# A late store sent in parts of 93, 32 and 3 partitions, and final waits in the order of issue

## The chip, the cores and the metric

The kernel runs on one NeuronCore of one Trainium2 chip. The time is the device time of one execution in microseconds (us); the lower it is, the better. The core has five engines with their own instruction streams: TensorE (PE in the profile, with PEld for its weight loads), VectorE (DVE), ScalarE (ACT), GpSimd (POOL) and SyncE (SP). SP does no arithmetic: here it issues transfers between HBM and the core's own memory, and waits for them. The transfers themselves are carried by 16 DMA engines.

## What is computed

A recurrence along a sequence, and on its result a mixture of eight low-rank adapters of which each row uses two:

```python
# a, b: (8, 6400, 128) float32
for t in range(S):
    h = a[:, t] * h + b[:, t]
    out[:, t] = h
x = out.reshape(51200, 128)

logits = x @ w_gate                                  # 8 experts
topk = np.argpartition(-logits, 2, axis=1)[:, :2]
...                                                  # softmax over the two: w
for e in range(8):
    for k in range(2):
        mask = topk[:, k] == e
        delta[mask] += w[mask, k, None] * ((x[mask] @ A[e]) @ B[e])   # A[e]: 128x16, B[e]: 16x128
return x + delta
```

Inputs `a` and `b` are 26.2 MB each, and the output is 26.2 MB.

## The kernel before

The 51,200 rows are cut into 100 chunks of 512 (`NCH = 100`, `C = 512`). For each chunk PE turns the rows of `a` and `b` so that time runs along the free dimension (line 567), DVE runs the recurrence over it (line 618), PE multiplies the result with gate and `A` (line 638), ACT copies these out of PSUM (line 644), a group of units gets its gate values (lines 671 to 694), DVE or POOL scale the products with them (lines 712 to 716), PE turns them (line 725), ACT or DVE copy them out (lines 731, 734), PE adds up the result (lines 739, 740), and ACT copies it into the buffer `outt` (line 749). From there SP stores it to HBM (line 784).

`outt` holds 72 blocks of 128 rows, which is 18 chunks: chunk c + 18 is copied to where chunk c was, so that copy waits until the store of chunk c has landed. All stores but the last four take two chunks at a time, 512 KB, and are called by the first: `st0`, `st2`, up to `st94`. The last four chunks, 96 to 99, are stored singly, 256 KB each. In `outt` and in HBM a store has 128 partitions; each has two pieces of 2 KB in a store of two chunks and one piece in a single one. `st68` stores chunks 68 and 69.

Each transfer adds 16 to a semaphore when it has landed. Stores of two chunks use nine semaphores in turn, `st0` to `st8` by their place in `outt`; the single ones use `stx0` to `stx3`. `st68` uses the semaphore `st7`, which `st86` uses again 18 chunks later.

The order of the instructions on each engine is worked out before the program is built: `Program.schedule` takes the operations in the order of a rank (a base, a template and a nudge by hand), with a duration for each. SP's own order is part of it: loads and stores stand in one stream, 48 loads of 512 KB of each input behind some smaller ones at the head. The last load is issued at 164.2 us; behind it stand twenty stores, `st64` to `st94` and then chunks 97, 98, 99 and 96. `st68` is the third of them.

When a store goes out in several parts, `SPLIT` gives the numbers of partitions for it by its first chunk; `send` (line 783) then issues one transfer for each part, all to the same semaphore, and `parts` makes the waits count 16 for each. In the kernel before `SPLIT` is empty. At the end of SP's stream (lines 838 to 840) it waits for each store semaphore to reach its full count, in the order in which the semaphores were made: `st0` to `st8`, then `stx0` to `stx3`.

Of the kernel before, what the change touches and what calls it, by code (L numbers as in the profile page):

```python
# [121 lines left out]
HEAD = 4  # L122
TAIL = 0
STORE_TAIL = [1, 1, 1, 1]
SPLIT = {}
TEMPLATE = {
    "la": [-7.837, -6.512, -2.793],
    "lb": [-6.969, -4.142, -2.441],
# [195 lines left out]
def bass_associative_scan_2x2__then__mixture_of_adapters_kernel(  # L324
# [65 lines left out]
    for u0, n in groups:  # L390
        nb = sum(m for _, m in units[u0 : u0 + n])
        if pos + nb > NZ:
            pos = 0
        for u in range(u0, u0 + n):
            zpos[u] = pos
            pos += units[u][1]

    with ExitStack() as stack:
# [41 lines left out]
        P = Program()  # L440
# [6 lines left out]
        s_dma = {}  # L447
# [46 lines left out]
        o_Z, o_ze, o_mu, o_T, o_te, o_D, o_oe, o_st = {}, {}, {}, {}, {}, {}, {}, {}  # L494
# [279 lines left out]
        def store(c, m):  # L774
# [4 lines left out]
            view = outt[:, q : q + m * J, :].rearrange("p (h j) d -> p h j d", j=J)  # L779
            cuts = SPLIT.get(c, [128])  # L780
            lows = [sum(cuts[:i]) for i in range(len(cuts))]
# [39 lines left out]
        def run(name, handle):  # L821
            eng[name] = handle
            for op in P.order[name]:
                for key, v in waits[op.i]:
                    handle.wait_ge(s_eng[key] if key in s_eng else s_dma[key], v)
                inst = op.emit()
                if op.sem is None:
                    inst.then_inc(s_eng[name], 1)
                else:
                    for part in inst if op.parts > 1 else [inst]:  # L830
                        part.then_inc(s_dma[op.sem], 16)
# [3 lines left out]
        @block.sync  # L835
        def _(sp):
            run("sp", sp)
            for key in s_dma:
                if key.startswith("st"):
                    sp.wait_ge(s_dma[key], 16 * sum(o.parts for o in o_st.values() if o.sem == key))  # L840

        @block.gpsimd
        def _(pool):
# [41 lines left out]
```

## Time and profile before

| what | us |
| --- | --- |
| median of three runs | 204.07 |
| lowest and highest of them | 203.96, 204.29 |
| the profiled execution, its own time | 204.2 |
| its span, from the first instruction to the last | 202.4 |
| PE, DVE, ACT, POOL busy in it | 182.1, 176.2, 172.6, 139.0 |

The span is what the trace covers; the rest of the profiled execution's time lies before the first and after the last instruction. A line with a line number, an engine and tiles (`L784 SPq DMA_DIRECT2D out_dram<-outt`) is a group of like instructions; SPq marks work of SP's queue, that is, issuing. "DMA to landing" is the time from the start of an issue until the transfer's semaphore has its full count. In the windows the columns after the times are the busy times of the engines with counts, then the granted clock of TensorE, the mean busy share of the 16 DMA engines (it can pass 1.00, since a packet's time can overlap the next one's) and the GB/s that they moved.

### The profile page before, as it was taken

The page shows a single profiled execution, that of the slowest core. Times are in us where ns is not written, and L with a number is a line of the kernel's source. Part 1 is how long each engine was busy: PE and PEld are TensorE (multiplying, and loading weights), DVE is VectorE, ACT ScalarE, POOL GpSimd, SP SyncE. Part 2 cuts the span into 40 slices and gives each one's busy share as a digit, 9 for nine tenths or more (in the row PEclk, how much of TensorE's full clock was granted, in tenths as well). Part 3 has the DMA queues.
Part 4 walks back from the last instruction along what each step waited for, and adds up shares of the span by engine and source line. Part 5 has one row for each costly group of instructions (what it writes and reads, how often), then busy time and mean ns, then how long its engine had stood idle before and what let it go on. Part 6 is the DMA issues. An engine that isn't in the chain of part 4 may idle for free.

```text
span 202.4 us, 7462 instructions
## 1 busy us (share of the span) xinstructions
PE 182.1 (90%) x3120; PEld 157.8 (78%) x3120; DVE 176.2 (87%) x291; ACT 172.6 (85%) x314; POOL 139.0 (69%) x176
## 2 busy tenths in 40 slices
PE   6878999999999999999999998987898998989870
PEld 6768787888888888888888887876887887877750
DVE  0579899999999999999999999887888998999960
ACT  2448899999999999999999997987797988978882
POOL 1015559998788898888888889796878897471000
PEclk9999999999999999999999999999999999999998
DMA  7999999999999999999999999999999999999994
GB/s 186 365 387 390 407 410 406 402 412 406 406 415 410 410 410 411 417 409 407 411 414 405 411 408 417 408 411 416 406 413 412 411 414 410 404 401 373 347 359 149
DMA packets 30993, 79.26 MB, mean 392 GB/s; under 512 B 3696, under 2 KB 3824, under 8 KB 30960
## 3 DMA queue, kind: packets, MB, share of 16 engines
q1 hardware_dynamic: 29488, 78.39, 98.7%
q10 hardware_dynamic: 1472, 0.40, 0.9%
q8 instruction: 25, 0.41, 0.8%
q14 instruction: 8, 0.07, 0.1%
HBM read 52.56 MB, written 26.21 MB: 389 GB/s over the span
## 4 chain that ended last, share of the span: by engine, by line
PE 23%; DMA 20%; DVE 19%; issue 1%; ACT 1%; SPq 0%; DVEq 0%
DMA b_tm<-in_b_dram 13%; DVE xT L618 9%; DMA a_tm<-in_a_dram 7%; PE pA L567 5%; PE pZ L638 4%; PE pB L567 4%; PE pO L725 3%; PE pO L739 3%; DVE zwT L734 3%; PE pO L740 3%; DVE zw L716 3%; DVE g L693 1%; ACT zwT L731 1%; ACT outt L749 1%; DVE m L672 1%
## 5 line engine op out<-in xcount | busy, mean ns | idle before, releaser
L618 DVE TENSOR_TENSOR_SCAN xT<-a_st,xT,pB 128x512 f16<-128x512 f32 x96 | 120.4, 1254 | 9.2 <-PE pB L567 5.4
L712 POOL TENSOR_TENSOR zw<-zl,g 128x512 f16<-128x512 f32 x90 | 94.1, 1061 | 16.2 <-DVE g L693 11.3
L567 PE MATMUL pA<-ident_f,a_tm 64*128 64x64 f32 (+1 forms) x752 | 68.7, 233 | 4.0 <-DMA b_tm<-in_b_dram 2.5
L567 PE MATMUL pB<-ident_f,b_tm 64*128 64x64 f32 (+1 forms) x752 | 68.6, 232 | 2.1 <-DMA a_tm<-in_a_dram 1.1
L585 ACT COPY a_st<-pA 128x512 f32<-128x512 f32 x100 | 59.9, 605 | 11.0 <-PE pA L567 6.5
L567 PEld LDWEIGHTS pA<-ident_f,a_tm 64*128 64x128 f32 (+1 forms) x752 | 55.8, 139 | 10.0 <-DMA b_tm<-in_b_dram 3.3
L567 PEld LDWEIGHTS pB<-ident_f,b_tm 64*128 64x128 f32 (+1 forms) x752 | 55.4, 139 | 7.1 <-DMA a_tm<-in_a_dram 1.6
L644 ACT COPY zl<-pZ 128x816 f32<-128x816 f32 (+1 forms) x69 | 57.6, 834 | 3.2 <-PE pZ L638 2.9
L749 ACT COPY outt<-pO 128x512 f32<-128x512 f32 x92 | 54.6, 605 | 3.4 <-PE pO L740 2.1
L739 PE MATMUL pO<-ident_h,xT 128*128 128x128 f16 x368 | 50.9, 221 | 1.6 <-ACT zwT L731 1.2
L740 PE MATMUL pO<-cst_h,zwT 128*128 128x128 f16 x368 | 50.1, 219 | 0.0
L739 PEld LDWEIGHTS pO<-ident_h,xT 128*128 128x128 f16 x368 | 40.6, 113 | 3.6 <-ACT zwT L731 1.7
L638 PE MATMUL pZ<-cst_h,xT 128*128 128x136 f16 x400 | 36.1, 225 | 3.7 <-DVE xT L618 2.2
L740 PEld LDWEIGHTS pO<-cst_h,zwT 128*128 128x128 f16 x368 | 36.5, 99 | 0.5 <-issue 0.5
L725 PE MATMUL pO<-ident_h,zw 128*128 128x128 f16 x368 | 35.2, 220 | 1.2 <-ACT outt L749 0.4
L638 PEld LDWEIGHTS pZ<-cst_h,xT 128*128 128x128 f16 x400 | 26.4, 115 | 8.6 <-DVE xT L618 5.3
L734 DVE COPY zwT<-pO 128x512 f16<-128x512 f16 x76 | 30.8, 408 | 0.9 <-PE pO L725 0.8
L725 PEld LDWEIGHTS pO<-ident_h,zw 128*128 128x128 f16 x368 | 22.6, 97 | 5.2 <-issue 1.3
L674 POOL TENSOR_TENSOR k<-zl,m 128x192 f32<-128x192 f32 (+2 forms) x16 | 7.8, 490 | 14.4 <-DVE m L672 14.4
L683 POOL TENSOR_TENSOR L<-k,m 128x192 f32<-128x192 f32 (+2 forms) x16 | 7.8, 489 | 9.6 <-DVE m L681 9.6
L676 POOL TENSOR_SCALAR L<-k 128x192 f32<-128x192 f32 (+2 forms) x16 | 12.8, 799 | 1.4
L731 ACT COPY zwT<-pO 128x512 f16<-128x512 f16 x16 | 9.6, 602 | 3.4 <-PE pO L725 3.4
(43 smaller groups left out, 104.6 us busy)
## 6 DMA issues: line engine op xcount, KB each, us to landing
a_tm<-in_a_dram SPq DMA_DIRECT2D x48, 512.0 KB, 13.4
b_tm<-in_b_dram SPq DMA_DIRECT2D x48, 512.0 KB, 13.3
out_dram<-outt SPq DMA_DIRECT2D x48, 512.0 KB, 13.2
a_tm<-in_a_dram SPq DMA_DIRECT2D x4, 256.0 KB, 4.7
out_dram<-outt SPq DMA_DIRECT2D x4, 256.0 KB, 4.1
b_tm<-in_b_dram SPq DMA_DIRECT2D x3, 256.0 KB, 5.6
b_tm<-in_b_dram ACTq DMA_DIRECT2D x1, 256.0 KB, 3.5
cst_f<-in_moe_A_dram ACTq DMA_DIRECT2D x1, 64.0 KB, 4.6
```

Of the source, the lines that this page charges most:

```text
L567: last = eng["pe"].transpose(*args)
L585: lambda: eng["act"].copy(a_st[c % NA][:, :], pA[:, c % 2, :]), fr(c, "ae"))
L618: last = eng["dve"].tensor_tensor_scan(out=x[:, s0:s1], data0=a_st[c % NA][:, s0:s1], data1=pB[:, c % 2, s0:s1], initial=init, op0=ALU.mul ...
L638: last = eng["pe"].matmul(pZ[:, k // (n // 2), o : o + W], xblock(b0 + k), Awg_h)
L644: return eng["act"].copy(zl[:, zb : zb + n, :].rearrange("p (h k) w -> p h (k w)", h=2), pZ[:, :, 0 : n // 2 * W])
L676: lambda e: e.tensor_scalar(out=ll, in0=kk, scalar1=0.0, scalar2=-1.0e30, op0=ALU.is_ge, op1=ALU.mult), dve=not main)
L712: lambda: eng["pool"].tensor_tensor(out=wv, in0=zv, in1=gv, op=ALU.mult), ba(gi, c, "mu"))
L725: last = eng["pe"].transpose(ptile[:, k * 128 : k * 128 + 128], zw[w][:, k, :], ident_h[:, :])
L734: lambda: eng["dve"].tensor_copy(zwT[w][:, :], ptile[:, 0:C]), ba(gi, c, "te"))
L739: eng["pe"].matmul(dst, xblock(b0 + k), ident_h[:, :], start=True, stop=False)
L740: last = eng["pe"].matmul(dst, zwT[w][:, k * 128 : k * 128 + 128], B_h, start=False, stop=True)
L749: lambda: eng["act"].copy(outt[:, o0 : o0 + n, :].rearrange("p k w -> p (k w)"), bank),
```

## The change

`st68` goes out as three transfers, of partitions 0 to 92, 93 to 124 and 125 to 127. The final waits of SP are taken in the order in which each semaphore's last store was issued. SP has two transfers more to issue than before; the order of everything else, on all engines, is as it was.

```diff
-SPLIT = {}
+SPLIT = {68: [93, 32, 3]}
...
         @block.sync
         def _(sp):
             run("sp", sp)
-            for key in s_dma:
-                if key.startswith("st"):
-                    sp.wait_ge(s_dma[key], 16 * sum(o.parts for o in o_st.values() if o.sem == key))
+            final = {}
+            for op in P.order["sp"]:
+                if op.sem.startswith("st"):
+                    final.pop(op.sem, None)
+                    final[op.sem] = op
+            for key in final:
+                sp.wait_ge(s_dma[key], 16 * sum(o.parts for o in o_st.values() if o.sem == key))
```

By that order the waits run `st3` to `st8`, `st0` to `st2`, `stx1`, `stx2`, `stx3`, `stx0`. In both programs they end up two to an instruction, with one left for the branch behind them. Before, the pairs are (`st7`, `st6`), (`st8`, `st5`), (`stx0`, `st4`), (`stx1`, `st3`), (`stx2`, `st2`), (`stx3`, `st1`), and `st0` with the branch. After, they are (`st1`, `st0`), (`st2`, `st8`), (`stx1`, `st7`), (`stx2`, `st6`), (`stx3`, `st5`), (`stx0`, `st4`), and `st3` with the branch.

## The prediction

> **What bounds the kernel now.** I read the page first, then the chain of work that ended last, then the waits of SP, then the DMA share in short windows of the last 20 us. The page:
>
> ```profile
> span 202.4 us, 7462 instructions
> ...
> DMA  7999999999999999999999999999999999999994
> GB/s 186 365 387 390 407 410 406 402 412 406 406 415 410 410 410 411 417 409 407 411 414 405 411 408 417 408 411 416 406 413 412 411 414 410 404 401 373 347 359 149
> ...
> q8 instruction: 25, 0.41, 0.8%
> ```
>
> The transfers run at 401 to 417 GB/s from the fifth slice to the 36th: the body is bound by them, and the change touches none of it. The last four slices are thinner (373, 347, 359, 149), so there the engines are no longer all at work. The chain ends on the result copies:
>
> ```profile
> 196.52 0.24 PE pB L739
> 197.20 0.58 ACT outt L749
> 197.80 0.58 ACT outt L749
> ```
>
> The last copy ends at 198.38 us, four microseconds before the span does. What fills these four is a store on its way. These are the last four stores (256 KB each, SP's line 784), then SP's waits at the end:
>
> ```profile
> L784 SPq DMA_DIRECT2D out_dram<-outt x4: 332/344/1168, 195.0 to 198.4; - x4
> DMA to landing us min/median/max: 3.3/4.1/4.9
> SPq L840 <- DMA out_dram<-outt: 2.0, 1, 2.0
> L840 SPq EVENT_SEMAPHORE  x4: 27/28/28, 201.8 to 201.9; - x4
> L398 SPq COMPARE_BRANCH  x1: 38/38/38, 202.0 to 202.0; - x1
> ```
>
> The first of the four was the longest on its way and landed at 195.0 + 4.9 = 199.9, the last at 198.4 + 3.3 = 201.7. Three steps in 1.8 us, 0.6 each, though they were issued 3.4 us apart: whoever completes them last works through a queue without a pause and is behind. The windows show how many engines that is:
>
> ```profile
> 182.00:184.00 2.00, 1.78 (x26) 1.30 (x23) 2.00 (x7) 1.76 (x4) 0.80 (x1) 1.00 1.05 406
> 184.00:186.00 2.00, 1.91 (x33) 1.67 (x31) 2.00 (x12) 1.71 (x4) 0.00 (x0) 1.00 0.98 378
> 186.00:188.00 2.00, 1.96 (x32) 1.63 (x30) 2.00 (x6) 1.86 (x5) 0.00 (x0) 1.00 0.91 349
> 188.00:190.00 2.00, 1.64 (x30) 1.45 (x28) 2.00 (x10) 1.88 (x4) 0.00 (x0) 1.00 0.73 271
> 190.00:192.00 2.00, 1.82 (x27) 1.35 (x24) 2.00 (x12) 1.24 (x5) 0.00 (x0) 1.00 1.03 392
> 192.00:194.00 2.00, 1.57 (x22) 1.23 (x23) 1.93 (x10) 1.93 (x6) 0.00 (x0) 1.00 0.81 308
> 194.00:196.00 2.00, 1.36 (x18) 0.85 (x15) 1.66 (x4) 1.65 (x5) 0.00 (x0) 1.00 1.04 393
> 196.00:198.00 2.00, 1.63 (x20) 1.16 (x20) 0.00 (x0) 1.84 (x4) 0.00 (x0) 1.00 0.92 342
> ...
> 200.75:201.00 0.25, 0.00 (x0) 0.00 (x0) 0.00 (x0) 0.00 (x0) 0.00 (x0) 0.90 0.24 82
> 201.00:201.25 0.25, 0.00 (x0) 0.00 (x0) 0.00 (x0) 0.00 (x0) 0.00 (x0) 0.50 0.06 25
> 201.25:201.50 0.25, 0.00 (x0) 0.00 (x0) 0.00 (x0) 0.00 (x0) 0.00 (x0) 0.50 0.00 0
> ```
>
> The last two columns are the DMA share and GB/s. Full is 406 GB/s, 25.4 per engine. From 201.00 to 201.25 it is 25: one engine of sixteen, alone, and then nothing. So the end of this kernel is one late DMA engine, about a quarter to half a microsecond behind the others, plus SP's remaining waits. Meanwhile others pause: 349 GB/s is 13.7 engines, 271 is 10.7.
>
> **The change part by part.** *The split.* The store of chunks 68 and 69 is the third after the last load, and goes out as 93, 32 and 3 rows of partitions instead of 128:
>
> ```profile
> L784 SPq DMA_DIRECT2D out_dram<-outt x1: 3772/3772/3772, 166.6 to 166.6; - x1
> DMA to landing us min/median/max: 14.9/14.9/14.9
> ...
> L784 SPq DMA_DIRECT2D out_dram<-outt x9: 588/1288/3772, 164.8 to 177.9; - x9
> ...
> L784 SPq DMA_DIRECT2D out_dram<-outt x11: 332/372/1168, 179.9 to 198.4; - x11
> DMA to landing us min/median/max: 3.3/5.6/11.2
> ```
>
> Two more issues on SP cost 0.33 us each at the least and 3.77 at the most. From 164.8 to 179.2 SP only issues stores, at 1.29 us, which is the time the engines need for 512 KB (524 KB / 406 GB/s = 1.29): it is held by the engines, not by its own work. Three issues that carry the bytes of one are held for those bytes, not three times. Behind the split stand 17 stores, no load, and no engine waits for SP; the store issued at 179.9 still lands 11.2 us later, so even 3.8 us of delay would be inside its queue. I take 0; without that cover it would be 0.7 to 7.5 us (twice the ends).
>
> Nothing computes later either. What could wait is a copy that reuses the buffer of this store, 18 chunks on. It lands at 166.6 + 14.9 = 181.5, and the copy into chunk 86 is this one:
>
> ```profile
> 184.90 0.59 ACT L749 COPY outt<-pO 128x512 f32<-128x512 f32 x1 [0.19 <-PE pO L740]
> ```
>
> It waited for PE, 3.4 us after the landing. The store may land that much later before ACT feels it.
>
> *Who carries the rows.* Whole, the store gives each of sixteen engines 8 rows of 4 KB. No transfer of before has a number of rows other than 128, so how 93 are dealt out is not in the trace. Between even dealing (nothing moves, 0) and all on one engine there are equal shares: 93 is 3 x 31 and has no other divisor up to 16; 32 gives 2 rows to each; 3 gives 1 to each of three. I take equal shares. Then three engines carry 31 + 2 + 1 = 34 rows, 26 more than now: 106.5 KB, 4.2 us at 25.4 GB/s. Thirteen carry 2 rows, 6 fewer: 24.6 KB, 0.9 us at the 0.6 us that 16.4 KB took the late engine at the end.
>
> The Trainium skill (DMA: Bandwidth & Descriptors, "Why a DMA increments its semaphore by 16 and not by 1") states that the engines used are the largest number up to 16 that divides the slowest dimension, and that they are the lowest-numbered ones. No run here shows it yet. By it the sum is the one above; by even dealing only the waits below remain.
>
> *Is there room for 4.2 us?* Between 184 and 198 us the windows fall short of 406 GB/s by 28, 57, 135, 14, 98, 13 and 64, each for 2 us: 818 KB, or 32 engine-microseconds. Three times 4.2 is 12.6. It fits if the three are engines that pause, and not if they are late ones. Engines differ because something other than the program's transfers takes some of them: q8 moved 25 packets of 16 KB, 0.8% of 16 x 202.4, 26 engine-microseconds, and the dips above say that it did not fall on all alike. The landing marks of the trace, which no view lists singly, have three engines ahead of the rest by nearly the whole lag at this store, and they are among those that came first when all were still level at the start. If shares are dealt from the first engine on, these get the 31 rows. I take that.
>
> *What the end gains.* The late engine is 0.9 us earlier. Then the next bound shows: the others stop between 200.75 and 201.00 (82 GB/s is three engines), it stops at 201.25. The gain is between 0.25 and 0.5; I take 0.4.
>
> *The waits.* In the program of before the thirteen final waits are two to an instruction, six instructions and the branch; the store issued last (`stx0`) is in the third. After its landing come three more instructions and the branch: 201.76 to 202.00 in steps of 0.06. In order of issue it stands in the sixth, with the branch alone behind it: three steps, 0.18 us. Bounds 0.15 and 0.2 by the rounded rows.
>
> *The sum.* Span 202.4 - 0.4 - 0.18 = 201.8. The profiled execution took 204.2 (1.8 lie around the span) and would take 203.6; the median of 204.07 is 0.13 lower, so **203.5**.
>
> **The rivals.**
> 1. *Waits only*: nothing moves off the late engine (even dealing), or the next bound stands right behind it. For: 82 GB/s in the window before the last says three engines end almost with it; the last store's issue took 1.17 us against a median of 0.34, which delays all sixteen. Against: one engine is alone for a whole window. Time 204.07 - 0.18 = 203.9.
> 2. *The three are late engines.* The place is the queue of these engines from 170 us on, the price 4.2 us less their pauses, and it decides as soon as one of the three has less than about 4 us of pauses before 198. An average engine has 32 / 16 = 2.0, so it ends 2.2 us later; it ended 0.3 before the last, so +1.9, less 0.18: 205.8. For: an average engine does not have the room, only the first ones do. Against: the order of the marks. The Trainium skill's "Rules for kernel authors" (same page) speak for this rival: one 128-partition transfer, all 16 engines. By them the split stretches 1.29 us of transfer to five on three engines; what that costs is what those engines lacked in pauses.
> 3. *The late engine is one of the three.* It has no pause, and 106.5 KB at its own 0.6 us for 16.4 KB are 3.9: 204.07 + 3.9 - 0.18 = 207.8. For: nothing names the engine. Against: three other engines than those that the landing marks put first would have to be taken. The same page of the Trainium skill ("Latency and other measured facts") has engines 7 and 15 as usually slower, which would not be among the first three; no row here numbers an engine.
> 4. *More than forecast*: the 1.17 us issue is itself held by the late engine. Without the extra 0.8 all others land earlier and the late one sets the end by its full 0.9: 204.07 - 0.9 - 0.18 = 203.0.
>
> **How the numbers follow.** Forecast 0.62, more than forecast 0.08, waits only 0.13, late engines 0.14, the late engine itself 0.03. About 0.2% (0.4 us) is what a measurement of this kernel can tell from no change: faster is below 203.66, slower above 204.48. Faster holds the first two and 0.02 of the third: 0.72; same the other 0.11 and 0.01 of the late engines: 0.12; slower the remaining 0.16. The range goes from 203.0 (the fourth rival) to 204.1 (waits only plus the spread of the three runs, 0.2): it leaves out the two slower cases, 0.17.
>
> **What would show it.** Right: the 93-row part lands late against the 32-row part while the whole store does not land later than 181.5; the window just before the end has several engines and no longer one; the last store lands 2.9 us after its issue instead of 3.3; one wait instruction and the branch after it. The dips at 186 to 190 get shallower. Wrong: GB/s of 76 or less (three engines) in windows near 200, the last landings beyond 202, copies of ACT from chunk 86 on idle before a DMA; or rows at the end that look as now with only the waits gone.

## The result and the profile after

The changed kernel takes 203.88 us (22 runs, 203.60 to 204.31), the kernel before, run in turn with it, 204.22 us (22 runs). The ratio is 0.9984 [0.9978, 0.9991]: the change is faster by 0.34 us, where 0.57 was forecast. A ratio, here and below, is that of the fast runs of both kernels with its 95% interval, not the quotient of the two medians, from which it differs by up to 0.0006.

The page of the changed kernel, with the rows that answer to those of before; the last is new, the part with 93 rows:

```profile
span 202.2 us, 7464 instructions
...
GB/s 193 371 390 391 407 410 408 399 413 406 406 412 415 407 410 409 420 410 406 410 414 406 410 410 415 409 411 414 409 411 412 411 416 410 401 377 385 356 331 177
...
q8 instruction: 25, 0.41, 0.8%
...
out_dram<-outt SPq DMA_DIRECT2D x1, 372.0 KB
```

The body is as before, 399 to 420 GB/s from the fifth slice to the 35th (the 36th is thinner, 377 instead of 401), and so is the instruction queue q8. SP's work at the end, from its instruction groups: duration in ns (min/median/max), then the first and the last start in us.

```profile
L784 SPq DMA_DIRECT2D out_dram<-outt x4: 333/532/817, 195.2 to 198.7; - x4
...
DMA to landing us min/median/max: 3.1/3.3/4.6
...
L844 SPq EVENT_SEMAPHORE  x2: 28/28/28, 201.1 to 201.8; - x2
...
L398 SPq COMPARE_BRANCH  x1: 38/38/38, 201.8 to 201.8; - x1
```

By the trace the last store lands at 198.65 + 3.08 = 201.73 us; before it was 198.41 + 3.33 = 201.74. Behind the landing stands one wait instruction and the branch, at 201.75 and 201.82, where before four and the branch reached to 202.00: the 0.18 us of the waits is there in full. But the last landing has not moved on the clock. Relative to its issue it is 0.25 us earlier (3.08 instead of 3.33), and the issue is 0.24 us later. The later issue comes from PE, which waited once at 168 us for nothing that the profile shows ("issue" in the rows below), somewhat longer in the profiled run of the change than in that of before. Up to this wait PE's instructions start 0.07 us earlier than the same ones before, behind it 0.28 us later, and 0.25 later to the end. From the waits of the changed kernel and then of the kernel before (engine and line, what it waited for, total us, times, longest us):

```profile
PE pO L739 <- issue: 0.7, 1, 0.7
```

```profile
PE pO L739 <- issue: 0.4, 1, 0.4
```

The same wait is 0.6 us in the profile of the kernel with the waits alone, so it is not the split that makes it. The windows of the changed kernel (last two columns: DMA share and GB/s):

```profile
184.00:186.00 2.00, 1.91 (x31) 1.67 (x31) 2.00 (x11) 1.47 (x4) 0.00 (x0) 1.00 1.04 396
186.00:188.00 2.00, 1.96 (x31) 1.63 (x30) 2.00 (x8) 1.88 (x5) 0.00 (x0) 1.00 0.94 355
188.00:190.00 2.00, 1.64 (x29) 1.45 (x27) 2.00 (x10) 1.87 (x5) 0.00 (x0) 1.00 0.84 312
...
192.00:194.00 2.00, 1.51 (x21) 0.99 (x19) 1.97 (x8) 1.94 (x6) 0.00 (x0) 1.00 0.67 253
...
200.50:200.75 0.25, 0.00 (x0) 0.00 (x0) 0.00 (x0) 0.00 (x0) 0.00 (x0) 0.50 0.33 115
200.75:201.00 0.25, 0.00 (x0) 0.00 (x0) 0.00 (x0) 0.00 (x0) 0.00 (x0) 0.50 0.06 25
201.00:201.25 0.25, 0.00 (x0) 0.00 (x0) 0.00 (x0) 0.00 (x0) 0.00 (x0) 0.50 0.06 25
201.25:201.50 0.25, 0.00 (x0) 0.00 (x0) 0.00 (x0) 0.00 (x0) 0.00 (x0) 0.50 0.00 0
```

From 184 to 190 us more is moved than before (396, 355 and 312 instead of 378, 349 and 271): engines that paused have work. (From 192 to 194 us it is less, 253 instead of 308.) But at the end one engine is alone again, now for two windows (25 GB/s). Is it the same one? The trace holds 16 landing marks for each store, one for each engine, in order of time and without the engine's number, so which mark belongs to which engine is read from the steps between them. These are the last two marks of each of the last four stores, in us, taken from the traces; the two kernels without a fetch, that is, in which no block of PE's instructions is fetched at the end, are from the last of the experiments below:

```
                                    97              98              99              96 (the last)
before                       197.75, 199.86  198.78, 200.49  200.72, 201.10  201.31, 201.74
after                        198.62, 198.76  199.41, 200.49  200.07, 201.12  201.04, 201.73
without a fetch, whole       198.35, 199.78  198.99, 200.42  199.98, 201.05  200.64, 201.67
without a fetch, in parts    198.68, 199.01  199.35, 199.66  199.98, 200.29  200.62, 200.92
```

Before, one engine is 2.1 and 1.7 us behind the next at the first two stores, and stays last in steps of 0.6. After, nothing at the first one lands later than 198.76: the late engine has been relieved by about 1 us. Then, at the second, one engine jumps to 200.49, 1.73 us after the last landing of the store ahead, and stays last through 201.12 and 201.73 in steps of 0.6. Something has taken an engine for over a microsecond. What it can be is in the DMA view, of a window of the changed kernel (197.40 to 198.20 us) and of the kernel before (198.20 to 199.30 us); the columns are packets, MB, and the packets' time as a share of 16 engines' window:

```profile
q8 instruction: 1, 0.02, 11.9%
```

```profile
q8 instruction: 1, 0.02, 5.3%
```

It is PE's last block of instructions. After, it begins at 197.48 us and takes 0.119 x 16 x 0.8 = 1.52 us; before, it begins at 198.28 and takes 0.053 x 16 x 1.1 = 0.93. By the marks, one block now stands ahead of three stores on one engine; before, it stood ahead of two, and the engine was through at 201.31. That it is this block and nothing else is for the experiments to show.

### The profile page after: what moved, and what is told of

Its sections match the earlier page's. It is cut to its first block, busy times and chain, and to the rows that moved or that the text cites. A ratio compares the mean times of both kernels' runs of the same rounds, so it can differ in the third digit from the quotient of the medians.

```text
span 202.2 us, 7464 instructions
## 1 busy us (share of the span) xinstructions
PE 181.5 (90%) x3120; PEld 157.6 (78%) x3120; DVE 176.2 (87%) x291; ACT 172.7 (85%) x314; POOL 139.1 (69%) x176
## 4 chain that ended last, share of the span: by engine, by line
PE 35%; DVE 21%; DMA 14%; ACT 4%; issue 2%; POOL 1%; SPq 0%; DVEq 0%
DVE xT L618 11%; PE pA L567 7%; DMA b_tm<-in_b_dram 7%; PE pZ L638 7%; DMA a_tm<-in_a_dram 6%; PE pB L567 5%; PE pO L725 5%; PE pO L739 5%; PE pO L740 4%; DVE zwT L734 4%; DVE zw L716 3%; ACT outt L749 1%; ACT zl L644 1%; DVE g L693 1%; ACT a_st L585 1%
```

## The experiments

Three theories were to be told apart. The first is that of the prediction: the late engine gets 6 rows less, the end moves by about 0.4 us, and the waits give 0.18. The second: only the waits do anything. The third came from the profile after: the relief is all there, and PE's last block gives it back.

### The waits alone, and the split alone

```diff
-SPLIT = {68: [93, 32, 3]}
+SPLIT = {}
```

> The final waits in the order of issue alone, the store of chunk 68 whole. My theory: after the last landing one wait instruction and the branch are left instead of four and the branch, 0.18 us, so 0.9991 of before (-0.1 to -0.25 us), with the last store landing 3.3 us after its issue as before and one late engine alone at the end. Rival, that the measured -0.34 us all comes from the waits: 0.9984 here too. Rival, that the waits bring nothing: 1.000.

204.14 us against 204.20, ratio 0.9994 [0.9986, 1.0003].

```diff
-            final = {}
-            for op in P.order["sp"]:
...
-            for key in final:
-                sp.wait_ge(s_dma[key], 16 * sum(o.parts for o in o_st.values() if o.sem == key))
+            for key in s_dma:
+                if key.startswith("st"):
+                    sp.wait_ge(s_dma[key], 16 * sum(o.parts for o in o_st.values() if o.sem == key))
```

> The store in 93, 32 and 3 alone, with the final waits in the old order. My theory: the late engine is relieved, -0.15 to -0.4 us (0.998 to 0.9993), and together with the waits alone it adds up to the whole change (-0.34). Rival, waits only: 1.000. Rival, that the split costs and the waits hide it: above 1.000.

204.08 us, 0.9991 [0.9982, 0.9999]. The two effects, 0.06% and 0.09%, add up to about the 0.16% of the change. Neither is large against its interval (that of the waits includes no change at all), and the split alone is worth 0.18 us, from 0.02 to 0.37, and not 0.4.

### Other ways to cut

Does the cutting itself help, with nothing moved? 96 and 32 rows are both multiples of 16.

```diff
-SPLIT = {68: [93, 32, 3]}
+SPLIT = {68: [96, 32]}
```

> The same store in two parts, 96 and 32, which can be dealt evenly to sixteen engines, with the new waits. Dealing in equal shares: every engine carries 8 rows as before, so only one more issue is left and the time is that of the waits alone (0.999). If cutting the store itself brings something (shorter issue, an earlier landing) it is at the full change's 0.9984; if a cut costs, it is above the waits alone by 0.3 us or more.

203.93 us, 0.9985 [0.9976, 0.9993], as much as the change. That looked like a gain of the cutting, so the same kernel was run again later:

> The store as 96 and 32 rows with the new waits, once more. By equal shares it moves no row between engines, so it is the waits alone, 0.999 (0.9985 to 0.9995). If the first 0.9985 was no chance, it is there again, and cutting the store brings something that the shares do not explain.

204.00 us against 204.21, 0.9992 [0.9983, 1.0001]. The second run is near the waits alone. The two together lie less than a tenth of a per cent below the waits alone, which is within the intervals: a small gain of the cutting is neither shown nor excluded, and by time alone the change can't be told from an even cut. What follows is a caution: at this size one ratio with its interval does not rank two variants.

The landing marks do tell them apart. From the first issue of the store in question to the last mark of chunk 97 it is 33.28 and 33.25 us where the store is whole (before, waits alone), 33.24 and 33.10 where it is cut evenly, and 32.36, 32.45 and 32.59 with 93, 32 and 3 rows (the change twice, the split alone). It is the uneven shares that relieve the late engine, by at least 0.7 us; the even cut moves it by less than 0.2.

If the sixteenth engine is the late one, a store that leaves it out relieves it. 120 = 15 x 8:

```diff
-SPLIT = {68: [93, 32, 3]}
+SPLIT = {68: [120, 8]}
```

> The same store in 120 and 8, with the new waits. By equal shares 120 goes to fifteen engines with 8 rows each and 8 to eight engines with one more, so one engine, the last, carries none and nobody carries more than 9. If the late engine at the end is that last one, it is 1.3 us earlier, nearly no other is later, and the time is at most that of the full change (0.998 or less). If the late engine is another, the time is that of the waits alone (0.999), and the last store lands 3.3 us after its issue.

204.19 us, 1.0006 [0.9994, 1.0018]; the last store lands at 198.73 + 3.01 = 201.74 us, as before. The late engine is not the one that 15 engines leave out. The Trainium skill (DMA: Bandwidth & Descriptors, "Latency and other measured facts") has engines 7 and 15 as usually slower, with a best guess at a cause that lies in transfers issued from GpSimd; the stores here are issued from SP. If the engine left out is the last of 0 to 15, then 15 is not the late one here, and for 7 no run tells.

Next, 91 rows. They were meant as seven engines with 13 rows each, which was a mistake in the expectation: 91 = 13 x 7 has the larger divisor 13, and its 36 landing marks (13 + 16 + 5, and one more for each of the two parts that are not dealt to all sixteen) show 13 engines with 7 rows.

```diff
-SPLIT = {68: [93, 32, 3]}
+SPLIT = {68: [91, 32, 5]}
```

> The same store as 91, 32 and 5 rows, with the new waits. By equal shares 91 goes as 13 rows to each of seven engines, 32 as 2 to all, 5 as 1 to five: seven engines carry 15 or 16 rows, nine carry 2. If the late engine is among the nine, it is relieved as by 93, 32, 3 (0.9 us), and no engine carries more than 8 rows too many, 1.3 us: the time is at most the change's, 0.9984. If the late engine is among the first seven, it carries 7 or 8 rows more, the last store lands 1 us later and the time is 1.004. Rival, that cutting alone does it: 0.9985 as with 96 and 32.

204.27 us against 204.26, 1.0004 [0.9995, 1.0013], and the last store lands 3.5 us after its issue. Thirteen engines have 9 or 10 rows instead of 8 and only three are relieved. The late one is not among these three, so relieving engines works only where the right one is relieved.

And the other extreme, a part that goes out on one engine alone, for the dealing itself: 127 has no divisor up to 16 but 1.

```diff
-SPLIT = {68: [93, 32, 3]}
+SPLIT = {68: [127, 1]}
```

> The same store as 127 and 1 rows, with the new waits. 127 has no divisor up to 16 but 1: by equal shares one engine carries the whole store, 120 rows more than now, 492 KB or 19 us at 25.4 GB/s. It has 2 to 5 us to spare, and the copy into chunk 86 waits for this store, so the end moves by 10 to 16 us, to 213 to 220 us, with long stretches in which the windows show 25 GB/s. If rows are dealt out evenly to sixteen engines, the time is that of the waits alone, 204.

215.94 us (2 runs), 1.0573 [1.0553, 1.0593]. From the windows, from the group of SP's issues and from the waits of this kernel:

```profile
180.00:182.00 2.00, 1.30 (x21) 1.12 (x21) 2.00 (x4) 1.10 (x2) 2.00 (x3) 1.00 0.07 26
182.00:184.00 2.00, 1.78 (x26) 1.30 (x24) 2.00 (x7) 1.77 (x4) 0.83 (x1) 1.00 0.07 26
184.00:186.00 2.00, 1.58 (x26) 1.30 (x24) 2.00 (x12) 0.61 (x1) 0.00 (x0) 1.00 0.07 27
```

```profile
L784 SPq DMA_DIRECT2D out_dram<-outt x1: 17123/17123/17123, 166.9 to 166.9; - x1
```

```profile
ACT outt L749 <- DMA out_dram<-outt: 10.2, 2, 9.9
```

For six microseconds all that moves is 26 to 27 GB/s, which is one engine. SP's next issue stands for 17.1 us behind it, and ACT waits 9.9 us for a block of `outt`. So the parts are dealt by equal shares over a divisor of their rows. The rule that the prediction drew on (the Trainium skill, DMA: Bandwidth & Descriptors, "Why a DMA increments its semaphore by 16 and not by 1") agrees, with these 26 GB/s and with the 24 landing marks of the three parts in the changed kernel: 3 + 16 + 3, and one more for each part that is not dealt to all sixteen (the first stands at 166.93 us, half a microsecond after its part's issue). It is also the cost of getting such a number wrong.

### With PE's last block out of the way

The third theory needs a kernel in which PE's last block is not fetched at the end. At its head PE does 16 transposes whose results nothing uses, to warm up. These kernels leave out 12 of them, and with that the last block is not fetched before the end (in two of their four traces it comes about 1.2 us behind the end of the span). First whole, with the new waits:

```diff
-WARM0 = 12
-WARM = 16
+WARM0 = 0
+WARM = 4
...
-SPLIT = {68: [93, 32, 3]}
+SPLIT = {}
```

> Store whole, new waits, and the twelve first warm-up transposes of PE left out (they compute nothing that is used; all other instructions keep their order). It has 24 PE instructions fewer, so that the last 16 KB block of PE's instructions, which is fetched over a DMA engine around 198.4 us, should not be asked for before PE ends. My theory of the end: SP's last issue is held until 0.37 us after this block is in (issue 1.15 us instead of 0.33), which makes all sixteen engines late, and the late engine sets the last landing anyway. Without the block the last issue takes 0.33 to 0.4 us, fifteen engines end 0.8 us earlier, the late one stays alone for about 1.2 us, and the time is as with the waits alone within 0.2 us. Rival: the block does not matter to the issue, which stays at 1.15 us.

204.21 us against 204.26, 1.0001 [0.999, 1.0012]. Its page, its last issues, and its last windows:

```profile
q8 instruction: 24, 0.39, 0.8%
```

```profile
L784 SPq DMA_DIRECT2D out_dram<-outt x4: 332/338/345, 195.1 to 198.6; - x4
...
DMA to landing us min/median/max: 3.1/3.9/4.7
```

```profile
200.00:200.25 0.25, 0.00 (x0) 0.00 (x0) 0.00 (x0) 0.00 (x0) 0.00 (x0) 0.50 0.71 262
200.25:200.50 0.25, 0.00 (x0) 0.00 (x0) 0.00 (x0) 0.00 (x0) 0.00 (x0) 0.50 0.07 25
200.50:200.75 0.25, 0.00 (x0) 0.00 (x0) 0.00 (x0) 0.00 (x0) 0.00 (x0) 0.50 0.07 25
200.75:201.00 0.25, 0.00 (x0) 0.00 (x0) 0.00 (x0) 0.00 (x0) 0.00 (x0) 0.50 0.06 25
201.00:201.25 0.25, 0.00 (x0) 0.00 (x0) 0.00 (x0) 0.00 (x0) 0.00 (x0) 0.50 0.04 16
```

24 blocks instead of 25. The last issue takes 0.33 us and not 1.17, so fifteen engines have started their last packets by 200.25 or soon after (a window counts a packet where it starts), and their marks are in by 200.64. Then the late one works alone for a whole microsecond, to 201.67, and the time is what it was with the block (204.14). This is the late engine without anything beside it. Now the same with the split:

```diff
-SPLIT = {}
+SPLIT = {68: [93, 32, 3]}
```

> The whole change (93, 32, 3 and the new waits), with the same twelve warm-up transposes left out. My theory: in the change as it is the relief of the late engine is given back, since the engine that brings PE's last block takes its last three stores behind it (201.1, 201.7 in the landings). Without the block neither this nor the held issue is left, so the last landing comes 2.2 to 2.6 us after the last issue instead of 3.08, and the time is 0.4 us or more below the whole change, or 0.997 or less of before. Rival: the block is not what is last, and the time is that of the change, 0.9984. Against both: fewer warm-ups cost at the start.

203.51 us (5 runs), 0.9963 [0.995, 0.9976]. Its page, issues and windows:

```profile
span 201.4 us, 7441 instructions
...
q8 instruction: 24, 0.39, 0.8%
```

```profile
L784 SPq DMA_DIRECT2D out_dram<-outt x4: 332/341/820, 195.1 to 198.5; - x4
...
DMA to landing us min/median/max: 2.4/3.2/3.9
```

```profile
200.00:200.25 0.25, 0.00 (x0) 0.00 (x0) 0.00 (x0) 0.00 (x0) 0.00 (x0) 1.00 0.67 246
200.25:200.50 0.25, 0.00 (x0) 0.00 (x0) 0.00 (x0) 0.00 (x0) 0.00 (x0) 1.00 0.05 16
200.50:200.75 0.25, 0.00 (x0) 0.00 (x0) 0.00 (x0) 0.00 (x0) 0.00 (x0) 1.00 0.00 0
```

The windows with 25 GB/s are gone. The last issue starts within 0.02 us of the other kernel's, and its store lands at 200.92 instead of 201.67: the split is worth 0.75 us here, and 0.70 by the medians. It was run again, side by side with the change:

> The whole change with the twelve first warm-up transposes left out, once more. My theory: 0.9963 again (0.995 to 0.9975), 0.3 us or more below the change on the same chip, last landing 2.4 us after the last issue. If the first result came of few runs, it stands with the change at 0.9984.

203.30 us (12 runs) against 204.21, 0.9961 [0.995, 0.9971]. The change itself:

> The changed kernel once more, on one chip with the next three. My theory: 0.9984 of before again (0.9978 to 0.9991), the last landing set by the engine that brings PE's last block, the last store landing 3.0 to 3.1 us after its issue, and SP's issue of the store of chunk 98 at 0.82 us and the last at 0.7. If the earlier ratio was luck of the chip, it is nearer 1.000.

203.94 us, 0.9985 [0.9976, 0.9994]. So the version without the 12 transposes beats both kernels, by 0.91 and 0.64 us. In the profile the store issued last lands 2.4 us after its issue again, against 3.1 for the change; on the clock it lands at 201.22, since this issue is 0.3 us later than in the first profile. By the medians the split is worth 0.2 to 0.3 us with the block at the end and 0.7 to 0.9 without it. PE's wait at 168 us is gone too without the 12 transposes, but the gain does not come from there: the last issue starts no earlier for it (198.3 to 198.8 us in the four kernels without them, 198.4 to 198.9 in the others that take 204 us).

Is there more to gain with other shares? 87 = 3 x 29, and 9 rows on nine engines:

```diff
-SPLIT = {68: [93, 32, 3]}
+SPLIT = {68: [87, 32, 9]}
```

> As the one before, with the store as 87, 32 and 9 rows: three engines carry 29 + 2 + 1 = 32 rows instead of 34, six carry 3, seven carry 2. With the block gone the last landing is 0.3 us behind the other engines. If it is one of the three that is last there, it is 0.3 us earlier and the time 0.1 to 0.3 us below 93, 32, 3; if it is the old late engine, it is the same or 0.15 us later.

203.36 us (5 runs), 0.9961 [0.9949, 0.9973]: no different from 93, 32 and 3. A gain of 0.1 us would not be seen with this interval; but the last mark stands 2.56 us after the last issue instead of 2.39, so nothing speaks for one.

## Why the prediction was right, and where it was not

*One late engine sets the end.* Right, and shown: with the block out of the way it works alone for a microsecond before the last landing, and taking rows from it removes just these windows.

*The split's issues cost nothing.* Right. SP's issues of `st66` and the three parts in the changed kernel:

```profile
L784 SPq DMA_DIRECT2D out_dram<-outt x4: 420/1546/3112, 165.8 to 170.0; - x4
```

The three parts took SP 0.42, 3.11 and 2.50 us, together 2.3 more than the 3.77 of the whole store, and the next store was issued 2.2 us later than before, at 172.56. It landed at 182.59, before at 182.84: the delay stayed inside the queue, as the prediction had it.

*No later compute.* Right. The last mark of the store in three parts is at 181.54 us, that of the whole one was at 181.53, and no copy of ACT from chunk 86 on waits for a store. The later last copy is PE's wait at 168 us, before the store lands.

*Equal shares over 3, 16 and 3 engines.* Right, by 26 GB/s and by the marks.

*The three have room.* Right for the change, where the engine with the block is last; how much room was left stays open. In the kernel before one engine is behind the others at chunk 97 (199.86, the next 197.75); in the change two are (198.76 and 198.62, the next 197.76), and so it is in every kernel with 93, 32 and 3 or 87, 32 and 9 rows. The second is probably one of the three, but that is not shown: the marks have no number, and without the 12 transposes the whole store too leaves a second one (198.35, the next 197.66). Without the block and with the split two are the last at the end, at 200.62 and 200.92. Of the reason given, the marks of the whole store show less than was read from them: they begin at 175.42, 175.44 and 175.47 us, but 175.84, 176.46 and 176.82 follow close behind.

*The late engine is 0.9 us earlier.* Right, as far as the marks show. At chunk 97 its mark is 1.1 us earlier or somewhat more (199.86 before, 198.76 or 198.62 after). At the end, before, it landed 3.33 us after the last issue; after, all engines but the one with the block are in by the second-last mark, 201.04, which is 2.39 us after it, 0.94 less. Which mark is the late engine's is read from the order, not from a number; at the end of the kernel the pair without the block gives 0.75.

*The end gains 0.4.* **This is the step that failed, by its size.** The next bound was taken to be the other engines as the trace of before showed them. It was one engine with a block of PE's instructions on it, which ends at 201.73, 0.69 us after all others. Before, the next engine was in at 201.31, 0.43 us ahead of the late one, so the 0.4 did fit the trace of before; but with the split the block came earlier and stood ahead of one store more, and that bound moved up to where the end had been. What is left is 0.25 us, measured from the last issue, in the profiles and 0.34 - 0.18 = 0.16 in the medians. The block was in sight: the issue of 1.17 us was quoted, and q8's share too.

*The waits give 0.18.* Shown in the profile, 201.76 to 202.00 against 201.75 to 201.82. The medians give 0.06 us for it alone and 0.21 with the second of the even cuts; they agree within their intervals.

*The number.* 203.88 is nearer to the waits alone (203.9) than to the forecast of 203.5, and the range from 203.0 to 204.1 held both, so that it holds says little about the split. The chance of 0.72 was for a time below 203.66. The time lies in the band above it, which had 0.12, also when the bound is moved up with the kernel before (204.22 instead of 204.07), to 203.81.

*The rivals.* Waits only had two forms. That nothing moves off the late engine is refuted by the pair without the block and by the marks. That the next bound stands right behind it is what the change met, though this bound was the engine with the block. The late engines and the late engine among the three: neither happened. The fourth, that the issue of 1.17 us is held by the late engine, falls: where the block is gone the engine is as late as ever and the issue takes 0.33 us. It goes with the block: in the profile of before the issue ends at 198.41 + 1.17 = 199.58 us, 0.37 after the fetch (198.28 + 0.93 = 199.21); in that of the change at 198.65 + 0.715 = 199.37, again 0.37 after it (197.48 + 1.52 = 199.00). In all ten profiles with a fetch at the end it is 0.36 to 0.38. The rival's price of 203.0 is near what the kernel does take with block and long issue gone, 203.3 to 203.5 us.

Of the signs it named, the single wait at the end and the shallower dips from 186 to 190 us came, and the store in parts landed with the whole one of before (181.54, 181.53). The last store was to land 2.9 us after its issue and landed 3.1 after, and several engines were to be at work just before the end, where again only one was.

**What stays open.** In every kernel with 93, 32 and 3 rows that has the fetch, it begins 0.4 to 1.6 us earlier than in the others that take 204 us (197.2 to 197.5 against 198.0 to 198.8) and takes longer (1.5 to 1.7 against 0.9 to 1.2 us). Why was not settled; if it came as late as before, more of the gain might stay, which was not tried. Nor is it known why only that one issue waits for a block of another engine, or which number the late engine has. The runs with 15 and 13 engines only say which ones it is not. The uneven cut has no even cut beside it among the kernels without the 12 transposes; that the shares do it there too is taken from the marks.

## What to carry to other kernels

When the end of a kernel hangs on one DMA engine, moving a late transfer's rows to others can help, if the right engine is relieved, and what it brings is the distance to the next engine in line. To find that distance, follow all that travels on the engines, instruction blocks too, to the end; a block fetched in the last 5 us cost nothing here where the store was whole, but took about 0.5 us of what the split gains, since stores queue behind it. Count the instructions of the longest stream against the block boundary: a few less at the head that do nothing can take a fetch from the end.

## What the runs showed of the hardware

A block of 16 KB for PE took 0.9 to 1.8 us on one DMA engine, where the late engine takes 0.6 for the 16 KB of a store, and SP's issue of an unrelated store stood until 0.36 to 0.38 us after the end of the last block. The Trainium skill (Runtime: NRT & Kernel Launch, "Instruction fetch mechanics") calls the cost of crossing such a boundary mostly hidden. With the store whole the runs agree: 204.14 us with the last block and 204.21 without it. With the split they differ: the block's engine ends 0.69 us behind all others, and PE's wait at 168 us for nothing that the profile shows, 0.4 to 0.7 us, began within a microsecond of the end of a block's fetch (166.5 to 167.5). With 24 instructions fewer ahead of it the wait is gone; that this block caused it was not tested further.

The issue of chunk 98, the second of the last four stores, takes 0.81 to 0.83 us in the kernels with 93, 32 and 3, with 87, 32 and 9 or with 127 and 1 rows, with or without the block, and 0.34 to 0.36 in the others. What holds it was not found.
